# Transform on one core: first step stored part by part, last step in float32 for every batch, first additions on VectorE, row copies on ScalarE

## The chip, the cores and the metric

The kernel runs on one core of one Trainium2 chip. The metric is the device time of one execution, in microseconds (us). Three timed executions of the kernel before took 641.56 us in the median (640.28 to 647.61). The engines are TensorE (PE in the profile, PEld for its weight loads), VectorE (DVE), ScalarE (ACT), GpSimd (POOL) and SyncE (SP, which issues DMAs here).

## The reference

What is computed is the real part of a two-dimensional Fourier transform of 8 batches of 3072 x 256 numbers, and after it two layers of eight experts on the 24576 rows. The layers choose experts by gates that are computed from the rows, so no expert can start before gates are there.

```python
X = np.fft.fft(x, axis=1); X = np.fft.fft(X, axis=2); x = X.real      # 8 x 3072 x 256
# first layer: gates from x @ w_gate, normalised over rows and experts
out += P[:, e:e+1] * (np.maximum(x @ w1[e], 0) @ w2[e])               # for each expert e
# second layer: each row goes to its best expert alone
out[mask] = gate * eom * (np.maximum(x[mask] @ w1[e], 0) @ w2[e])
```

## The kernel before

The change lies in the transform, `fft()` (line 234), which runs the 8 batches one after the other. Symmetry leaves 65 values of k1 and 24 real parts for each, 1560 numbers per column of a batch. For one batch the stages are these.

- `load` (line 250): four DMAs bring the batch, in chunks of 4, 3, 4 and 2 values of n2, from SP's queue into four buffers `xin`.
- `fold` (line 281): additions that use the symmetry, on each chunk. Line 291 adds the first and third, second and fourth parts of `xin` into `P` (1040, 780, 1040 and 520 numbers per partition in the four chunks), on GpSimd except for two chunks of the first batch. Lines 293 to 299 are six more additions and subtractions on VectorE, over `E` into `ab`.
- `stage1` (line 301): the first step. 13 float32 products per half of a batch, with `ab` as the stationary operand and the table `T` as the moving one, and eight copies on ScalarE (line 315) that bring 390 numbers each from PSUM into `Y`. `Y` holds 65 values of k1 with the 24 parts of each side by side, so each copy writes numbers that stand 24 words apart.
- `stage2` (line 317): for each of 13 groups of 5 values of k1, two float32 products (line 326) that take 120 columns of `Y`, side by side, as the stationary operand, and the table `CAB` with 146 columns as the moving one. A float32 product appears as two weight loads and two matmuls in the trace, so 13 groups are 52 of each. For batches 0 to 4 ScalarE then copies 32 gate columns into `Gc` (line 330) and 275 columns into `Z`, rounded to fp32r (line 339), and VectorE subtracts the rounded part from PSUM, which leaves the rest in `Zl` (line 340). Batches 5 to 7 (`late`) have one plain copy of all 292 columns into `Z` (line 328).
- `stage3` (line 344): the last step, on two groups at a time. For batches 0 to 4 it makes six fp32r products of 256 or 258 columns (line 358: high by high, high by low, low by high, for two halves). The result is copied into `row` (line 364), for two of three pairs on VectorE, and a DMA writes the rows out. For batches 5 to 7 the products are float32 ones of 127 or 129 columns, one group at a time, and are put off into a later wait: `product` and `tick` (lines 361 and 363) issue them between steps of the gate work.
- `logits` (line 384): the gates of a batch.

Between batches 4 and 7 the token lists are made (lines 446 to 458). A scheduler orders the instructions of all engines from the order of the code, dependences and its own estimate of time. Buffers limit how far stages run ahead: two of each `Y`, one of each `ab`, two PSUM tiles for stage 1, three for stage 2, two for stage 3. After the transform `moe()` runs the experts; its code is not changed. One line of it serves as a measure below: line 778 copies logits out of the token table, where they stand 12 words apart (`LW`); line 1284, in the experts, reads and writes numbers that stand side by side.

Of the kernel before, what the change touches and what calls it, by code (L numbers as in the profile page):

```python
# [10 lines left out]
F32 = mybir.dt.float32  # L11
# [9 lines left out]
K1, NJ, GP = 65, 24, 13          # kept k1 values, real parts per k1, k1 groups of 5 per batch  # L21
RP = 120                         # rows of a group: 5 k1 x 24 k2
XW = 256                         # row of the spectrum buffer: U[128], U[0:128] (even m, odd m), V[1:128] (even, odd)
AW = 272                         # row of the results of the first part: the values, and their share of the second gate's logits
ZW = 292                         # half-transformed row: the same and gate columns
LW = 12                          # row of the token table: 8 logits, output row, spectrum row and sign in two parts, place
TS = (18, 4, 6)                  # token tiles of the compact path: from all but the last LATE + 1 batches, one batch more, and the rest
# [3 lines left out]
DUMP = 640                       # rows that take the unused slots  # L31
N0 = 384                         # early pairs of the first expert: picked before the last batches
C1 = (256, 472, 464, 408, 360, 328, 320, 288)    # (other) pairs of the compact path, experts by falling count
N2 = (448, 256)                  # early pairs of the second part's first experts: from rows that the last experts of the first part leave alone
C2 = (256, 288, 416, 384, 288, 336, 320, 192)
KS = 5                           # experts of the first part before those
SIGN = 2.0 ** 16                 # marks the second sign in a column's number
MW = 480                         # widest unit (and four groups of rows of the general path)
GS = 4                           # token tiles of a group
NS = (12, 0, 1, 2, 3, 4, 5, 6, 7, 8, 9, 10, 11)   # kept n2 values  # L40
CH = ((0, 4), (4, 3), (7, 4), (11, 2))
DEFER = 3                        # batches whose last transform step fills the wait for the gates
LATE = 2                         # batches that the early tokens and the order of the experts do not wait for
ZF = 1
ZA = 2
SC = 2.0 ** 100
# chains of steps: from the last products of a chain to a step's own, and these (us); None: a step without products
# [12 lines left out]
PW = {1: (1, 3, 4, 5), 2: (2, 3, 4)}  # experts whose low weight parts GpSimd takes  # L60


# ---------------------------------------------------------------- host side
def host_consts(B):
    NC = 2 * GP * B
# [17 lines left out]
    # columns: [gate U even | U128 | U even] [gate V even | - | V even]; [U odd | gate U odd | -] [V odd | gate V odd | -]  # L83
# [22 lines left out]
    for i in range(5):  # L106
        M3[i * 24:i * 24 + 24, 0, i * 24:i * 24 + 24] = MU
        M3[i * 24:i * 24 + 24, 1, i * 24:i * 24 + 24] = MV
# [13 lines left out]
    k1p = 5 * np.arange(GP)[None, :] + p[:, None] // 24  # L122
# [13 lines left out]
    # per row of the spectrum buffer and sign: output row, 2*row+sign; mirrored duplicates  # L136
# [3 lines left out]
    k = 5 * g[None, :] + (pr // 24)[:, None] + 128 * (pr % 24)[:, None]  # L140
# [6 lines left out]
    kk = 5 * g[None, :] + (pr // 24)[:, None]  # L147
# [28 lines left out]
# ---------------------------------------------------------------- device side  # L176
def through(steps):
    """all steps of a generator at once; its result"""
    while True:
        try:  # L180
            next(steps)
        except StopIteration as e:
            return e.value


class Kernel:
# [46 lines left out]
    # ------------------------------------------------------------ spectrum  # L233
    def fft(self, ctx, zp, p3, pq):
        """fills Xd and the token table; returns the steps left over: the last transform of some batches"""
# [42 lines left out]
        AB, Y, Z, Zl, Gc = {}, {}, {}, {}, {}  # L278
        M3h = zp.tile([128, 2, RP], F32R, name="M3h")
        M3l = zp.tile([128, 2, RP], F32R, name="M3l")  # L280

        def fold(b, c):
# [8 lines left out]
            (nc.vector if b == 0 and c % 2 == 0 else nc.gpsimd).tensor_tensor(out=P[:, :n], in0=xv[:, :n, :, 0], in1=xv[:, :n, :, 1], op=ALU.add)  # L291
# [9 lines left out]
        def stage1(b, g):  # L301
            if g == 0:
                for h in range(2):
                    Y[b, h] = sp.tile([128, K1, NJ], F32, name=f"Y{b}_{h}", tag=f"Y{h}")
            for h in range(2):
                yv = Y[b, h].rearrange("p k (r n) -> p n r k", r=2)
# [10 lines left out]
        def stage2(b, g):  # L317
            late = b >= max(1, B - DEFER)
            if g == 0 and late:
                Z[b] = zp.tile([RP, GP, ZW], F32, name=f"Z{b}", tag="Z", bufs=DEFER)  # L320
            elif g == 0:
                Gc[b] = sp.tile([RP, GP, 2, 2, 8], F32, name=f"Gc{b}", tag="Gc", bufs=1)
            ps = p2.tile([RP, ZW], F32, name=f"p2_{b}_{g}", tag="p2")
            pv = ps.rearrange("p (u h w) -> p u h w", u=2, h=2)
            for h in range(2):
                nc.tensor.matmul(pv[:, :, h], Y[b, h][:, 5 * g:5 * g + 5].rearrange("p a j -> p (a j)"), CAB[:, h], start=True, stop=True)  # L326
            if late:
                nc.scalar.copy(out=Z[b][:, g], in_=ps)
                return
            nc.scalar.copy(out=Gc[b][:, g], in_=bass.AP(tensor=ps.tensor, offset=ps.offset, ap=[ps.ap[0], [146, 2], [137, 2], [1, 8]]))  # L330
            if g % 2 == 0:
                Z[b, g] = sp.tile([RP, ZW, 2], F32, name=f"Z{b}_{g}", tag="Zh", bufs=3)
                if g + 1 < GP:
                    Zl[b, g] = sp.tile([RP, ZW, 2], F32R, name=f"Zl{b}_{g}", tag="Zl", bufs=2)
            z, k = Z[b, g - g % 2][:, :, g % 2], g - g % 2
            if g == GP - 1:
                nc.scalar.copy(out=z[:, 8:283], in_=ps[:, 8:283])
            else:
                nc.scalar.copy(out=z[:, 8:283].bitcast(F32R), in_=ps[:, 8:283])
                nc.vector.tensor_tensor(out=Zl[b, k][:, 8:283, g % 2], in0=ps[:, 8:283], in1=z[:, 8:283], op=ALU.subtract)  # L340
# [3 lines left out]
        def stage3(b, g, m, row, g0, n, late):  # L344
            z = Z[b][:, g:g + m] if late else Z[b, g]
            pp, tag = (self.p4, "p4") if late else (p3, "p3")
            ps = pp.tile([RP, 2, XW], F32, name=f"p3_{b}_{g}", tag=tag)
            fine = not late and m == 2
            if not late:
                # the two groups by turns: float32r takes even counts only  # L350
                z, pi = z.rearrange("p w m -> p (w m)"), ps.rearrange("p m w -> p (m w)")
                ps = pi.rearrange("p (w m) -> p m w", m=2)
                zi, z = z, z.rearrange("p (w m) -> p m w", m=2)
            for uv in (1, 0) if fine else ():
                # V brings a column of zeros, which U writes after it: products of 256 columns
                o, i = (slice(256, 512), slice(310, 566)) if uv else (slice(0, 258), slice(16, 274))
                for q, (l, r) in enumerate(((M3h, zi.bitcast(F32R)), (M3h, Zl[b, g].rearrange("p w m -> p (w m)")), (M3l, zi.bitcast(F32R)))):
                    nc.tensor.matmul(pi[:, o], l[:RP, uv], r[:, i], start=q == 0, stop=q == 2)
            for k in range(0 if fine else m):
                for o, uv, i in ((slice(0, 129), 0, slice(8, 137)), (slice(129, 256), 1, slice(156, 283))):  # L360
                    (self.product if late else nc.tensor.matmul)(ps[:, k, o], M3[:RP, uv], z[:, k, i], start=True, stop=True)
                    if late:
                        self.tick(0.213)
            (nc.scalar.copy if late or g % 6 < ZA else nc.vector.tensor_copy)(out=row[:, g - g0:g - g0 + m], in_=ps[:, :m])
            if g + m == g0 + n:
                nc.sync.dma_start(out=Xv[:, b, g0 * XW:(g0 + n) * XW], in_=row[:, :n].rearrange("p c w -> p (c w)"))

        def rows(b, late):
            """steps of the last transform of a batch, with the groups that they finish"""
# [14 lines left out]
        def logits(b):  # L384
            L = self.L
            t = sp.tile([RP, 2, GP, 8], F32, name=f"lt{b}", tag="lt", bufs=1)
            for uv in range(2):
                g0, g1 = (Gc[b][:, :, uv, h] for h in range(2)) if b in Gc else (Z[b][:, :, o + 146 * uv:o + 146 * uv + 8] for o in (0, 137))
# [15 lines left out]
        nc.scalar.copy(out=M3h[:RP], in_=M3[:RP])  # L404
# [1234 lines left out]
```

## Time and profile before

| | before |
|---|---|
| timed, median of 3 | 641.56 us |
| the profiled execution's span | 655.9 us |
| PE busy | 552.0 us (84%) |
| DVE busy | 465.2 us (71%) |
| ACT busy | 314.0 us (48%) |
| POOL busy | 304.7 us (46%) |
| HBM over the span | 185 GB/s |

The profiled execution is one execution, with the profiler on; its own time on record is its span. The transform's products end near 200 us of it; what follows is the experts with the put-off products among them. The profile's tables that matter are the busy time of each engine by stretch, the groups of instructions by line with their mean duration, the waits, and the instructions in order of time.

### The profile page before, as it was taken

The page shows a single profiled execution, that of the slowest core. Times are in us where ns is not written, and L with a number is a line of the kernel's source. Part 1 is how long each engine was busy: PE and PEld are TensorE (multiplying, and loading weights), DVE is VectorE, ACT ScalarE, POOL GpSimd, SP SyncE. Part 2 cuts the span into 40 slices and gives each one's busy share as a digit, 9 for nine tenths or more (in the row PEclk, how much of TensorE's full clock was granted, in tenths as well). Part 3 has the DMA queues.
Part 4 walks back from the last instruction along what each step waited for, and adds up shares of the span by engine and source line. Part 5 has one row for each costly group of instructions (what it writes and reads, how often), then busy time and mean ns, then how long its engine had stood idle before and what let it go on. Part 6 is the DMA issues. An engine that isn't in the chain of part 4 may idle for free. (4 is left out here: it accounts for less than half of the span.)

```text
span 655.9 us, 10840 instructions
## 1 busy us (share of the span) xinstructions
PE 552.0 (84%) x3587; PEld 516.7 (79%) x3587; DVE 465.2 (71%) x1248; ACT 314.0 (48%) x730; POOL 304.7 (46%) x254
## 2 busy tenths in 40 slices
PE   3788878889747867999979967689879999999995
PEld 3678777878637867998869967689768998999994
DVE  6799999989627768996788446467657577356641
ACT  2677665768414643364433334334533255444641
POOL 3443433341653447324464788330443588781112
PEclk9999999999958996799978978959998999998999
DMA  9887778799614887898655456543751234454400
GB/s 341 328 280 245 269 233 276 223 306 352 229 14 146 256 259 235 273 355 279 214 132 177 55 115 174 102 87 101 220 100 41 57 111 164 132 196 147 158 22 29
DMA packets 67631, 121.90 MB, mean 186 GB/s; under 512 B 14108, under 2 KB 49498, under 8 KB 65519
## 3 DMA queue, kind: packets, MB, share of 16 engines
q1 hardware_dynamic: 40415, 89.41, 42.2%
q0 software_dynamic: 8672, 13.38, 10.0%
q10 hardware_dynamic: 18480, 18.35, 8.0%
q8 instruction: 30, 0.49, 0.3%
q14 instruction: 34, 0.28, 0.1%
HBM read 70.66 MB, written 50.71 MB: 185 GB/s over the span
## 5 line engine op out<-in xcount | busy, mean ns | idle before, releaser
L1285 DVE SCALAR_TENSOR_TENSOR hl<-ph,hh 128x256 fp32r<-128x256 f32 (+12 forms) x152 | 75.5, 505 | 62.9 <-ACT hh L1284 52.1
L1128 PE MATMUL ph<-xh,wh 128*128 128x256 f32 (+12 forms) x304 | 102.5, 341 | 5.7 <-DVE hl L1285 3.1
L1284 ACT ACTIVATE hh<-ph 128x256 fp32r<-128x256 f32 (+12 forms) x152 | 67.0, 453 | 82.6 <-PE ph L1128 69.7
L1128 PE MATMUL ph<-xl,wh 128*128 128x256 f32 (+12 forms) x304 | 101.3, 333 | 0.0
L1054 ACT CAST wh<-wr 128x512 fp32r<-128x512 f32 x128 | 72.7, 618 | 58.4 <-DMA wr<-w2a 19.5
L1128 PE MATMUL ph<-xh,wl 128*128 128x256 f32 (+12 forms) x304 | 100.0, 329 | 0.0
L291 POOL TENSOR_TENSOR P<-xin 128x1040 f32<-128x1040 f32 (+2 forms) x30 | 55.3, 1845 | 90.8 <-DVE E L294 73.5
L1128 PE MATMUL yt<-hl,wh 128*128 128x288 f32 (+11 forms) x240 | 82.8, 348 | 12.0 <-DVE hl L1285 12.0
L1055 POOL TENSOR_TENSOR wl<-wr,wh 128x512 fp32r<-128x512 f32 x56 | 72.2, 1344 | 35.5 <-ACT wh L1054 35.2
L315 ACT COPY Y<-p 128x390 f32<-128x390 f32 x64 | 68.2, 1159 | 34.5 <-PE p L314 29.4
L1128 PE MATMUL yt<-hh,wh 128*128 128x288 f32 (+11 forms) x240 | 78.3, 353 | 7.5 <-ACT yb L1343 5.2
L326 PE MATMUL p<-CAB,Y 128*120 128x146 f32 x416 | 70.4, 305 | 14.6 <-issue 11.3
L1128 PE MATMUL yt<-hh,wl 128*128 128x288 f32 (+11 forms) x240 | 81.8, 345 | 0.0
L1091 POOL DMA_INDIRECT Ad<-yb,it x29 | 49.3, 1701 | 56.2 <-ACT yb L1347 35.3
L326 PEld LDWEIGHTS p<-CAB,Y 128*120 128x120 f32 x416 | 58.8, 193 | 18.6 <-issue 12.9
L1128 PEld LDWEIGHTS ph<-xh,wh 128*128 128x128 f32 x304 | 60.1, 199 | 9.4 <-DVE hl L1285 4.8
L1055 DVE TENSOR_TENSOR wl<-wr,wh 128x512 fp32r<-128x512 f32 x72 | 47.6, 689 | 22.4 <-ACT wh L1054 18.4
L314 PE MATMUL p<-T,ab 128*128 128x130 f32 x352 | 53.1, 288 | 9.4 <-DVE ab L297 5.2
L1128 PEld LDWEIGHTS ph<-xl,wh 128*128 128x128 f32 x304 | 60.1, 198 | 1.0
L1128 PEld LDWEIGHTS ph<-xh,wl 128*128 128x128 f32 x304 | 59.9, 197 | 0.9
L1128 PEld LDWEIGHTS yt<-hl,wh 128*128 128x128 f32 x240 | 48.7, 203 | 14.2 <-DVE hl L1285 13.2
L314 PEld LDWEIGHTS p<-T,ab 128*128 128x128 f32 x352 | 45.1, 195 | 13.0 <-ACT Gc L330 2.8
(330 smaller groups left out, 1230.6 us busy)
## 6 DMA issues: line engine op xcount, KB each, us to landing
out<-zero ACTq DMA_DIRECT2D x35, 512.0 KB
xin<-xf SPq DMA_DIRECT2D x16, 1040.0 KB
Xd<-row SPq DMA_DIRECT2D x24, 480.0 KB
wr<-w1a SPq DMA_DIRECT2D x16, 512.0 KB
wr<-w2a SPq DMA_DIRECT2D x16, 512.0 KB
wr<-w1b SPq DMA_DIRECT2D x16, 512.0 KB
wr<-w2b SPq DMA_DIRECT2D x16, 512.0 KB
out<-zero SPq DMA_DIRECT2D x13, 512.0 KB
```

The costliest lines, as they stand in the source:

```text
L291: (nc.vector if b == 0 and c % 2 == 0 else nc.gpsimd).tensor_tensor(out=P[:, :n], in0=xv[:, :n, :, 0], in1=xv[:, :n, :, 1], op=ALU.add)
L314: nc.tensor.matmul(ps[:, q], AB[b, h][:, n2 + 1], T[:, n2], start=True, stop=True)
L315: nc.scalar.copy(out=yv[:, 3 * g:3 * g + 3], in_=ps.rearrange("p n (r k) -> p n r k", r=2))
L326: nc.tensor.matmul(pv[:, :, h], Y[b, h][:, 5 * g:5 * g + 5].rearrange("p a j -> p (a j)"), CAB[:, h], start=True, stop=True)
L1054: nc.scalar.copy(out=Wt["h" + k][:, s], in_=r)
L1055: eng.tensor_tensor(out=Wt["l" + k][:, s], in0=r, in1=Wt["h" + k][:, s].bitcast(F32), op=ALU.subtract)
L1091: ins = nc.gpsimd.indirect_dma_start(out=self.Ad, out_offset=off, in_=y, in_offset=None, compute_op=ALU.add, bounds_check=CAPT + DUMP - 1, ...
L1128: ins = self.nc.tensor.matmul(*args, **kw).ins
L1284: nc.scalar.activation(out=a[:, :w], in_=ph[:, :w], func=AF.Relu)
L1285: nc.vector.scalar_tensor_tensor(out=b[:, :w], in0=ph[:, :w], scalar=0.0, in1=a[:, :w].bitcast(F32), op0=ALU.max, op1=ALU.subtract)
```

## The change

Four things are changed. `Y` is stored part by part: 24 parts, each with its 65 values of k1 side by side. A group is no longer five neighbouring k1 but every 13th, so that the 120 columns of a group are every 13th number of `Y`; the tables that name rows (`M3`, `k1p`, the rows in `LC`) follow that. The split into a rounded part and a rest is gone: all batches have the one plain copy into `Z`, with one buffer more, and the last step is two float32 products for two groups, of 258 and 254 columns, for all batches. The first additions are on VectorE for all chunks. All copies into `row` are on ScalarE. Besides, comments are taken out, which shifts line numbers.

```diff
-        M3[i * 24:i * 24 + 24, 0, i * 24:i * 24 + 24] = MU
-        M3[i * 24:i * 24 + 24, 1, i * 24:i * 24 + 24] = MV
+        M3[i:RP:5, 0, i * 24:i * 24 + 24] = MU
+        M3[i:RP:5, 1, i * 24:i * 24 + 24] = MV
...
-    k = 5 * g[None, :] + (pr // 24)[:, None] + 128 * (pr % 24)[:, None]
+    k = g[None, :] + GP * (pr // 24)[:, None] + 128 * (pr % 24)[:, None]
...
-            (nc.vector if b == 0 and c % 2 == 0 else nc.gpsimd).tensor_tensor(out=P[:, :n], in0=xv[:, :n, :, 0], in1=xv[:, :n, :, 1], op=ALU.add)
+            nc.vector.tensor_tensor(out=P[:, :n], in0=xv[:, :n, :, 0], in1=xv[:, :n, :, 1], op=ALU.add)
...
-                    Y[b, h] = sp.tile([128, K1, NJ], F32, name=f"Y{b}_{h}", tag=f"Y{h}")
+                    Y[b, h] = sp.tile([128, NJ, K1], F32, name=f"Y{b}_{h}", tag=f"Y{h}")
...
-                yv = Y[b, h].rearrange("p k (r n) -> p n r k", r=2)
+                yv = Y[b, h].rearrange("p (r n) k -> p n r k", r=2)
...
-                nc.tensor.matmul(pv[:, :, h], Y[b, h][:, 5 * g:5 * g + 5].rearrange("p a j -> p (a j)"), CAB[:, h], start=True, stop=True)
-            if late:
-                nc.scalar.copy(out=Z[b][:, g], in_=ps)
-                return
-            nc.scalar.copy(out=Gc[b][:, g], in_=bass.AP(tensor=ps.tensor, offset=ps.offset, ap=[ps.ap[0], [146, 2], [137, 2], [1, 8]]))
...
-                nc.scalar.copy(out=z[:, 8:283].bitcast(F32R), in_=ps[:, 8:283])
-                nc.vector.tensor_tensor(out=Zl[b, k][:, 8:283, g % 2], in0=ps[:, 8:283], in1=z[:, 8:283], op=ALU.subtract)
+                nc.tensor.matmul(pv[:, :, h], Y[b, h].rearrange("p j k -> p (j k)")[:, g::GP], CAB[:, h], start=True, stop=True)
+            nc.scalar.copy(out=Z[b][:, g], in_=ps)
...
-            for uv in (1, 0) if fine else ():
-                o, i = (slice(256, 512), slice(310, 566)) if uv else (slice(0, 258), slice(16, 274))
-                for q, (l, r) in enumerate(((M3h, zi.bitcast(F32R)), (M3h, Zl[b, g].rearrange("p w m -> p (w m)")), (M3l, zi.bitcast(F32R)))):
-                    nc.tensor.matmul(pi[:, o], l[:RP, uv], r[:, i], start=q == 0, stop=q == 2)
...
-            (nc.scalar.copy if late or g % 6 < ZA else nc.vector.tensor_copy)(out=row[:, g - g0:g - g0 + m], in_=ps[:, :m])
+            for o, uv, i in ((slice(0, 129), 0, slice(8, 137)), (slice(129, 256), 1, slice(156, 283))):
+                (self.product if late else nc.tensor.matmul)(ps[:, :m, o], M3[:RP, uv], z[:, :, i], start=True, stop=True)
+                if late:
+                    self.tick(0.213 * m)
+            nc.scalar.copy(out=row[:, g - g0:g - g0 + m], in_=ps[:, :m])
```

On TensorE, in batch 1, this stands before the change: products of the second step (L326, `p2_1_3` is batch 1, group 3) and of the last step (L358, `p3_1_0` is groups 0 and 1).

```order
L326 MATMUL p2_1_3_533<-CAB_99,Y1_0_431 120x2x73
L326 MATMUL p2_1_3_533<-CAB_99,Y1_1_432 120x2x73
L358 MATMUL p3_1_0_549<-Zl1_0_487,M3h_119 120x256
L358 MATMUL p3_1_0_549<-Z1_0_486,M3l_120 120x256
L358 MATMUL p3_1_0_549<-Z1_0_486,M3h_119 120x258
L358 MATMUL p3_1_0_549<-Zl1_0_487,M3h_119 120x258
L358 MATMUL p3_1_0_549<-Z1_0_486,M3l_120 120x258
```

With the change the same place reads as follows; L321 is the second step and L331 the last one.

```order
L321 MATMUL p2_1_3_457<-CAB_99,Y1_0_365 120x2x73
L321 MATMUL p2_1_3_457<-CAB_99,Y1_1_366 120x2x73
L331 MATMUL p3_1_0_471<-Z1_415,M3_101 120x2x129
L331 MATMUL p3_1_0_471<-Z1_415,M3_101 120x2x127
L321 MATMUL p2_1_4_475<-CAB_99,Y1_0_365 120x2x73
```

The second step's products stand where they stood, with the new stationary operand; six products of the last step (the first of the six stands a little ahead) have become two, and no remainder `Zl` is waited for.

On VectorE, while batch 1 is in the second step and batch 2 is folded, this stands before the change (L340 is the remainder, L293 and L294 write `E`, L296 to L299 write `ab`).

```order
L340 TENSOR_TENSOR Zl1_0_487<-p2_1_0_482,Z1_0_486 120x275
L293 TENSOR_TENSOR E2_1_509<-P2_1_507 128x3x130
L340 TENSOR_TENSOR Zl1_0_487<-p2_1_1_501,Z1_0_486 120x275
L294 TENSOR_TENSOR E2_1_509<-P2_1_507 128x3x130
L398 TENSOR_TENSOR L_67<-lv0_422,misc_63 120x13x8
L340 TENSOR_TENSOR Zl1_2_521<-p2_1_2_516,Z1_2_520 120x275
L296 TENSOR_TENSOR ab2_0_490<-E2_1_509 128x3x65
```

With the change it reads as follows; L289 is the addition that GpSimd made, L291 to L297 are the fold.

```order
L297 TENSOR_TENSOR ab2_1_421<-E2_1_437 128x3x64
L289 TENSOR_TENSOR P2_3_461<-xin2_3_403 128x520
L291 TENSOR_TENSOR E2_2_450<-P2_2_448 128x4x130
L292 TENSOR_TENSOR E2_2_450<-P2_2_448 128x4x130
L294 TENSOR_TENSOR ab2_0_420<-E2_2_450 128x4x65
```

VectorE no longer stands between the second and the last step; its queue holds the fold and its first addition, which is put one chunk ahead of the fold that needs it.

## Rows read from the trace of the kernel before

**Rows 1.** The page, part 1: busy us, share of the span, instructions.

```profile
PE 552.0 (84%) x3587; PEld 516.7 (79%) x3587; DVE 465.2 (71%) x1248; ACT 314.0 (48%) x730; POOL 304.7 (46%) x254
```

**Rows 2.** Busy time by stretch (start:end, length, engines, clock, DMA share, GB/s).

```profile
core 0: us, PE busy (x) PEld busy (x) DVE busy (x) ACT busy (x) POOL busy (x), PEclk, DMA share, GB/s
0.00:23.30 23.30, 10.15 (x61) 9.13 (x61) 15.59 (x35) 9.20 (x11) 9.82 (x12) 1.00 0.95 355
23.30:143.30 120.00, 100.46 (x769) 92.99 (x770) 117.85 (x253) 79.55 (x193) 45.46 (x26) 1.00 0.79 260
143.30:175.00 31.70, 29.30 (x237) 28.11 (x236) 29.32 (x119) 24.75 (x54) 9.24 (x9) 1.00 1.04 347
175.00:193.00 18.00, 6.17 (x23) 4.54 (x22) 3.55 (x17) 2.12 (x6) 13.67 (x14) 0.60 0.12 14
```

**Rows 3.** Waits, 23.3 to 143.3 us: total, times, longest.

```profile
POOL P L291 <- DVE E L294: 70.5, 23, 5.0
...
PE p L311 <- DVE ab L297: 6.0, 6, 1.5
PE p L314 <- DVE ab L297: 5.0, 5, 1.6
```

**Rows 4.** Groups of instructions, 23.3 to 143.3 us: busy, mean ns | idle before.

```profile
L340 DVE TENSOR_TENSOR Zl<-p,Z 120x275 fp32r<-120x275 f32 x60 | 24.7, 432 | 3.8 <-ACT Z L339 3.8
L296 DVE TENSOR_TENSOR ab<-E 128x260 f32<-128x260 f32 x12 | 16.6, 1380 | 0.0
...
L364 DVE COPY row<-p 120x512 f32<-120x512 f32 x20 | 13.5, 675 | 0.0
```

**Rows 5.** In order of time (start us, us): one addition beside GpSimd's, one without.

```profile
84.72 0.79 DVE L340 TENSOR_TENSOR Zl<-p,Z 120x275 fp32r<-120x275 f32 x2
84.93 2.04 POOL L291 TENSOR_TENSOR P<-xin 128x1040 f32<-128x1040 f32 x1 [3.33 <-DVE E L294]
85.42 1.82 DVE L296 TENSOR_TENSOR ab<-E 128x260 f32<-128x260 f32 x1
...
95.21 0.42 DVE L296 TENSOR_TENSOR ab<-E 128x260 f32<-128x260 f32 x1
```

**Rows 6.** Groups: the first addition where it is on VectorE already.

```profile
L291 DVE TENSOR_TENSOR P<-xin 128x1040 f32<-128x1040 f32 x2 | 2.5, 1238 | 4.7 <-DMA xin<-xf 4.7
```

**Rows 7.** TensorE: the second step's group, then products in order of time.

```profile
L326 PE MATMUL p<-CAB,Y 128*120 128x146 f32 x260 | 42.0, 291 | 2.6 <-ACT Y L315 1.5 <-DVE Zl L340 1.0
...
85.92 0.28 PE L358 MATMUL p<-Z,M3l 120*120 120x256 f32 x1
...
86.28 0.28 PE L358 MATMUL p<-Z,M3l 120*120 120x258 f32 x1
...
153.43 1.66 PE L326 MATMUL p<-CAB,Y 128*120 128x146 f32 x12
```

**Rows 8.** Weight loads in order of time.

```profile
144.20 0.76 PEld L314 LDWEIGHTS p<-T,ab 128*128 128x128 f32 x6
...
153.32 1.54 PEld L326 LDWEIGHTS p<-CAB,Y 128*120 128x120 f32 x12
```

**Rows 9.** Groups on ScalarE: words apart (L315, L778) and side by side.

```profile
L315 ACT COPY Y<-p 128x390 f32<-128x390 f32 x44 | 46.6, 1166 | 20.4 <-PE p L314 15.5 <-PE p L326 4.3
L364 ACT COPY row<-p 120x512 f32<-120x512 f32 x10 | 6.0, 605 | 0.4
...
L778 ACT CAST R<-LcT 128x162 fp32r<-128x162 f32 x2 | 0.9, 484 | 0.0
L778 ACT CAST R<-LcT 128x54 fp32r<-128x54 f32 x2 | 0.5, 303 | 0.0
...
L1284 ACT ACTIVATE hh<-ph 128x472 fp32r<-128x472 f32 x8 | 4.5, 565 | 1.8 <-DVE hl L1285 0.7 <-PE ph L1128 0.6 <-issue 0.4
L1284 ACT ACTIVATE hh<-ph 128x256 fp32r<-128x256 f32 x8 | 3.1, 384 | 4.6 <-PE ph L1128 3.6 <-issue 1.0
```

More of the change, by code (lines that the diff above doesn't have):

```diff
@@ L44 @@
 ZF = 1
-ZA = 2
 SC = 2.0 ** 100
@@ L121, in host_consts @@
     colx = np.broadcast_to(SIGN * cs + cb * RP * GP + cg, (128, NC))
-    k1p = 5 * np.arange(GP)[None, :] + p[:, None] // 24
+    k1p = np.arange(GP)[None, :] + GP * (p[:, None] // 24)
     dup = np.where((k1p == 0) | (k1p == 64), -1e30, 0.0)
@@ L146, in host_consts @@
         LC[:, s, :, 1], LC[:, s, :, 2] = (2 * row + s) // 256 * 256, (2 * row + s) % 256
-    kk = 5 * g[None, :] + (pr // 24)[:, None]
+    kk = g[None, :] + GP * (pr // 24)[:, None]
     LC[:, 1, :, 0] = np.where((kk == 0) | (kk == 64), 1e6, LC[:, 1, :, 0])
@@ L276, in gate_cols @@
                     nc.vector.tensor_scalar(out=CAB[:, ab, uv, k], in0=ps, scalar1=msk[:, 2 * ab + uv:2 * ab + uv + 1], scalar2=None, op0=ALU.mult)
-        AB, Y, Z, Zl, Gc = {}, {}, {}, {}, {}
-        M3h = zp.tile([128, 2, RP], F32R, name="M3h")
-        M3l = zp.tile([128, 2, RP], F32R, name="M3l")
+        AB, Y, Z = {}, {}, {}
         def fold(b, c):
@@ L317, in stage2 @@
         def stage2(b, g):
[L318 to L322, printed above, removed]
+            if g == 0:
+                Z[b] = zp.tile([RP, GP, ZW], F32, name=f"Z{b}", tag="Z", bufs=DEFER + 1)
             ps = p2.tile([RP, ZW], F32, name=f"p2_{b}_{g}", tag="p2")
@@ L325, in stage2 @@
             for h in range(2):
-                nc.tensor.matmul(pv[:, :, h], Y[b, h][:, 5 * g:5 * g + 5].rearrange("p a j -> p (a j)"), CAB[:, h], start=True, stop=True)
-            if late:
-                nc.scalar.copy(out=Z[b][:, g], in_=ps)
-                return
-            nc.scalar.copy(out=Gc[b][:, g], in_=bass.AP(tensor=ps.tensor, offset=ps.offset, ap=[ps.ap[0], [146, 2], [137, 2], [1, 8]]))
[L331 to L338, printed above, removed]
-                nc.scalar.copy(out=z[:, 8:283].bitcast(F32R), in_=ps[:, 8:283])
-                nc.vector.tensor_tensor(out=Zl[b, k][:, 8:283, g % 2], in0=ps[:, 8:283], in1=z[:, 8:283], op=ALU.subtract)
+                nc.tensor.matmul(pv[:, :, h], Y[b, h].rearrange("p j k -> p (j k)")[:, g::GP], CAB[:, h], start=True, stop=True)
@@ L342, in fft @@
+            nc.scalar.copy(out=Z[b][:, g], in_=ps)
         Xv = self.Xd.rearrange("(b p c) w -> p b (c w)", p=RP, c=GP)
         def stage3(b, g, m, row, g0, n, late):
-            z = Z[b][:, g:g + m] if late else Z[b, g]
+            z = Z[b][:, g:g + m]
             pp, tag = (self.p4, "p4") if late else (p3, "p3")
             ps = pp.tile([RP, 2, XW], F32, name=f"p3_{b}_{g}", tag=tag)
[L348 to L353, printed above, removed]
@@ L354, in stage3 @@
-            for uv in (1, 0) if fine else ():
-                o, i = (slice(256, 512), slice(310, 566)) if uv else (slice(0, 258), slice(16, 274))
-                for q, (l, r) in enumerate(((M3h, zi.bitcast(F32R)), (M3h, Zl[b, g].rearrange("p w m -> p (w m)")), (M3l, zi.bitcast(F32R)))):
-                    nc.tensor.matmul(pi[:, o], l[:RP, uv], r[:, i], start=q == 0, stop=q == 2)
[L359 to L363, printed above, removed]
@@ L387, in logits @@
             for uv in range(2):
-                g0, g1 = (Gc[b][:, :, uv, h] for h in range(2)) if b in Gc else (Z[b][:, :, o + 146 * uv:o + 146 * uv + 8] for o in (0, 137))
+                g0, g1 = (Z[b][:, :, o + 146 * uv:o + 146 * uv + 8] for o in (0, 137))
                 nc.vector.tensor_tensor(out=t[:, uv], in0=g0, in1=g1, op=ALU.add)
@@ L403, in fft @@
             fold(0, c)
-        nc.scalar.copy(out=M3h[:RP], in_=M3[:RP])
-        nc.vector.tensor_tensor(out=M3l[:RP], in0=M3[:RP], in1=M3h[:RP].bitcast(F32), op=ALU.subtract)
         nc.gpsimd.tensor_copy(out=self.L[:, :, :, 8:12], in_=LC)
```

## The prediction, made before the changed kernel ran

> **What bounds the kernel now.** I read the busy time by stretch first, then the waits of the longest stretch, then the groups of instructions in it. Over the whole span PE is the busiest engine at 84% [rows 1], but that is a mean over stages. From 23.3 to 143.3 us (the early stretch: second and last step of batches 0 to 4, first step of batches 1 to 6, folds) DVE is busy for 117.85 of 120 us and PE for 100.46 [rows 2]. PE waits there for DVE's `ab`, for 6.0 and 5.0 us [rows 3], so DVE is the bound. From 143.3 to 175 us PE has 29.3 of 31.7 us, at the granted clock 1.00 (the 2.4 GHz level). From 175 to 193 us nearly everything stands still [rows 2]; the change touches nothing that I can connect with that. The change can win where DVE is the bound, and the question is what bounds instead.
>
> **The change part by part.**
>
> *VectorE.* It loses 60 remainders; two take 0.79 us and one of them 0.43 [rows 4, 5], so each holds the queue for 0.36 us: 21.6 us. It loses 20 row copies, 13.5 us [rows 4], some 13 without their overlap. It gains GpSimd's additions of the stretch, 13 of 1040 numbers, 7 of 780 and 6 of 520: one of 1040 takes 1.24 us [rows 6], so by size some 16 + 7 + 4 = 27 us. It also loses a wait that looks like work. While GpSimd adds (84.93, 2.04 us), the VectorE addition of 260 numbers that starts beside it takes 1.82 us, and alone 0.42 [rows 5]; the mean over 12 is 1.38 [rows 4], which is 11.5 us over, and the shorter forms of the same line make it some 17. Sum: 118 - 21.6 - 13 + 27 - 17 = 93 of 120 us. DVE is no longer the bound, and the loss of GpSimd's work costs nothing: all that waited for that engine was DVE. Bounds: 87 if the additions are as cheap by number as a fold's, 100 if part of the excess was not GpSimd's.
>
> *ScalarE.* The 44 copies into `Y` take 1.17 us each for 390 numbers; with numbers side by side 512 take 0.605 [rows 9], so 390 some 0.5: 29 us less. It loses the `Gc` copies and gains 20 row copies of some 0.5 us net, 10 us. From 79.55 busy us [rows 2] it comes to some 55, with room.
>
> *The last step on TensorE.* Six fp32r products follow each other at 0.12 us (85.92 to 86.28 is three of them), so 0.72 us for two groups. A float32 instruction of 146 columns comes every 0.125 us (12 in 1.66 us, less one of 0.29, by 11) [rows 7]. Two products of 258 and 254 columns are four instructions, by columns 0.22 us each: 0.88. Thirty pairs cost 30 x 0.16 = 4.8 us more. In the put-off batches there are half as many instructions of twice the columns: nothing.
>
> *The second step's weight loads* are the unknown, and they decide. Today 120 columns of `Y` stand side by side; afterwards 13 words lie between one and the next. The trace of before has no weight load of that kind. Six loads of 128 columns take 0.76 us, so they follow at 0.114 or less, and those of 120 columns at some 0.105. They lie behind matmuls of 0.125: the 12 loads take 1.54 us, at the matmuls' pace [rows 8]. Lower bound: the loads stay under 0.125, cost nothing. The nearest rows for words apart are ScalarE's. Reading numbers 12 words apart, 162 take 484 ns and 54 take 303: 1.68 ns a number. Side by side, 472 take 565 and 256 take 384: 0.84 ns. That is twice. Upper bound: the copy into `Y` writes 24 words apart and takes 1166 ns for 390 [rows 9], which after some 0.15 us of start is 2.6 ns a number, three times. So a load takes 0.105, 0.21 or 0.31 us. I take twice, some 0.2, as the read is the closer relative; then the load, not the matmul, sets the pace of the second step.
>
> The Trainium skill speaks against the change here: SBUF — State Buffer, section Door 1 (a note on "cachelines" in it), says that an access goes at full bandwidth only while at least two fall on the same 16-byte line, which in float32 allows a step of up to four words. ScalarE's rows, at twice the time, agree; no run here shows it for weight loads yet. By that rule alone the second step slows and the sum is the one at 0.2 below.
>
> *The sum.* PE's instructions of the early stretch before: second step 260 x 0.125 = 32.5; first step 240 instructions of 130 columns at 0.114 and 48 short ones at 0.11, 32.6; last step 180 x 0.12 and 20 single ones, 24; gates 2. That is 91, and 96 with the new last step. Loads at 0.2 add 260 x 0.075 = 19.5, less 30 x 0.075 = 2 where a load lies behind a product of 0.22 us: 113. Where nothing but PE bounds, from 143.3 to 175 us, PE has 92% [rows 2]; I take 0.93 to allow for its waits. 113 / 0.93 = 121 us against 120: what DVE gives, the weight loads take, +1. Behind it, batches 5 to 7 hold another 156 instructions of the second step in stretches that PE fills, and have no last step there. They cost 156 x 0.075 = 12 us, of which some 2 lie in the standstill: +10. Before 23.3 us, and after 200, nothing of weight changes. Together +11 us. The profiled span of 655.9 us is 14.3 above the median of 641.56; the stretches concerned ran at full granted clock, so I carry microseconds over as they are: 641.6 + 11 = 653.
>
> **The rivals.**
>
> *The weight load stays hidden* (faster). Its mechanism: the load reads slower than it can, its pace coming from the array and not from the buffer, so that a read at half the rate still fits behind a matmul of 0.125 us. For it: fp32r products of 256 columns come every 0.12 us [rows 7], so PE can read a number in 0.47 ns on its other operand, and loads at 0.88 ns have slack of nearly two. Against it: that is a read side by side. Then the early stretch takes 96 / 0.93 = 103 us in place of 120, at most 17 to 18 less, and the late one is as before: 624. The DMA does not forbid that: the stretch moves 260 GB/s x 120 us = 31 MB, 88 us at the 355 GB/s of the start [rows 2]. The load time from which this decides: the early gain of 18 is eaten when (230 / 0.93 + 133) x (load - 0.125) = 18, at 0.173 us. Below that the kernel is faster than before, above it slower.
>
> A rule that gives this result is in the Trainium skill, TensorE: Matmul & The Clock Gate, section LDWEIGHTS: the time of a load depends on the number of columns alone, columns divided by 1.2 in ns. For 120 columns this is an estimate of 100 ns, close to the 105 above; it does not speak of steps, and no row here shows one.
>
> *Three times* (much slower). The load pays as the copy into `Y` does, 0.31 us. Then the early stretch has 96 + 260 x 0.185 - 30 x 0.09 = 141, at 0.95 for the loads' steadier pace 149, +29, and the late one 133 x 0.185 = 25, less a little cover, +22: 692.
>
> *DVE stays the bound.* If none of the excess was GpSimd's doing, DVE has 110 of 120 us, and at loads of 0.2 the sum stays at 653, at hidden loads it is 641.6 - 10 = 632. I give it no chance of its own; it narrows the faster case.
>
> **How the numbers follow.** Loads at 0.18 to 0.23 us: 0.52, time 653, its own range 645 to 664. Hidden loads: 0.28, time 624, 618 to 634. Three times: 0.13, time 692. In between, about 0.15 to 0.175: 0.07, time 632 to 645. The prediction is that of the likeliest, 653. The range reaches from 618, the whole of the faster case, to 668 and leaves out the third case and a little: 618 to 668. About 1% is what a measurement of this kernel can tell from no change, 635 to 648. Faster: the hidden case and a little of the one between, 0.29. Same: the rest between and the lower end of the likeliest, 0.19. Slower: 0.52.
>
> **What would show it.** Second-step weight loads of 120 columns in a run of their own follow each other at 0.2 us (right), 0.12 (hidden) or 0.3 (three times). VectorE has under 100 us where it had 118, and its addition of 260 numbers takes 0.42 us at the mean. ScalarE's copy into `Y` takes about 0.5 us. PE has no waits for `ab` to speak of, and its gaps lie between loads. The last step's instructions follow at 0.22 us. The end of the transform moves by some 11 us, and the experts behind it keep their time. The prediction is wrong if the loads are at another pace, if the first additions come late for the fold behind copies into `L` or gates on VectorE, or if the time after the transform changes.

## The result, and the profile after

| | before | after |
|---|---|---|
| timed, median of 4 | 643.89 us (640.28 to 647.61) | 652.00 us (651.17 to 653.60) |
| ratio | 1 | 1.0138, 95% interval 1.0093 to 1.0184 |
| the profiled execution's span | 655.9 us, in a second trace 636.4 us | 649.7 us |

The changed kernel is slower by 1.4%: 8 us by the medians, 9 by the ratio. Before has a fourth execution here, of 646.23 us. The prediction was 653, and slower.

The trace of before that stands ahead of the prediction was an unlucky one. Its standstill from 175 to 193 us [rows 2] did not come back in a second trace of the same kernel (experiment 1 below). With that standstill the transform's last gates end at 199.8 us in the first trace, later than the 197.9 us of after. Where time points are compared, the second one stands for before. Its span of 636.4 us belongs to an execution of 638.2 us, near the low end of what before takes, so a difference of two spans is some microseconds larger than the timed one.

The page of after, part 1 (busy us, share of the span, instructions), answers to [rows 1]:

```profile
PE 578.8 (89%) x3455; PEld 545.7 (84%) x3455; DVE 431.1 (66%) x1197; ACT 290.3 (45%) x684; POOL 245.2 (38%) x224
```

PE is busy for 26.8 us longer than in the first trace of before, with fewer instructions; VectorE, ScalarE and GpSimd are all relieved. The busy time by stretch of after, with the stretches and columns of [rows 2]:

```profile
23.30:143.30 120.00, 120.00 (x690) 116.46 (x690) 83.33 (x198) 65.45 (x145) 0.00 (x0) 1.00 0.78 254
143.30:175.00 31.70, 31.60 (x191) 31.40 (x189) 21.45 (x75) 15.79 (x42) 4.44 (x5) 1.00 1.07 359
175.00:193.00 18.00, 17.90 (x86) 17.72 (x86) 11.78 (x63) 7.17 (x23) 12.07 (x13) 1.00 0.16 27
```

In the early stretch VectorE fell from 117.85 to 83.33 us, and PE rose from 100.46 to all of the 120, at the granted clock 1.00 (the 2.4 GHz level). The bound has moved from VectorE to PE. The waits of after in the same stretch (total, times, longest) say so from the other side:

```profile
ACT Z L322 <- PE p L321: 27.9, 57, 1.8
DVE ab L294 <- PE p L312: 19.5, 5, 7.4
ACT row L334 <- PE p L331: 16.5, 28, 1.6
ACT Y L313 <- PE p L312: 10.1, 30, 1.9
```

In [rows 3] PE waited for VectorE's `ab`; now the four longest name PE as the one that is waited for (the next, 9.8 us, is VectorE waiting for ScalarE's copy into `Z`). VectorE waits for PE to be done with the `ab` that it wants to write over.

What fills PE is seen in the groups of the page of after (busy us, mean ns | idle before), here the second step's weight loads and matmuls:

```profile
L321 PEld LDWEIGHTS p<-CAB,Y 128*120 128x120 f32 x416 | 104.9, 337 | 1.1 <-ACT Y L313 0.3
L321 PE MATMUL p<-CAB,Y 128*120 128x146 f32 x416 | 109.5, 401 | 0.1
```

A matmul of 146 columns takes 401 ns in the mean of the whole run; before it took 291 in the early stretch [rows 7]. Its form is the same; it waits for its weights. In order of time, the first six loads of a run of eight, and their matmuls:

```profile
73.64 1.51 PEld L321 LDWEIGHTS p<-CAB,Y 128*120 128x120 f32 x6
...
73.75 1.61 PE L321 MATMUL p<-CAB,Y 128*120 128x146 f32 x6
```

Six loads in 1.51 us, less one of 0.341 (their median duration), over five gaps: one every 0.234 us. Over all runs of such loads the median from start to start is 0.240 us. In [rows 8] twelve took 1.54 us, which is 0.124.

The end of the early stretch's work and of the transform's is marked by the gates of batch 4 and of batch 7 (L392 before, L362 after). Their last rows in the second trace of before, start and duration in us:

```profile
145.09 0.36 PE L392 MATMUL pl<-lt,M 120*120 120x104 f32 x2
...
181.16 0.87 PE L392 MATMUL pl<-lt,M 120*120 120x104 f32 x4
```

The same two places of after:

```profile
146.87 0.36 PE L362 MATMUL pl<-lt,M 120*120 120x104 f32 x2
...
196.95 0.99 PE L362 MATMUL pl<-lt,M 120*120 120x104 f32 x4
```

Batch 4 is done 1.8 us later, batch 7 15.9 us later. So the early stretch costs 2 us and the late one 14. From the last gate to the end there are 636.4 - 182.0 = 454.4 us before and 649.7 - 197.9 = 451.8 after: the experts keep their time to 3 us.

### The profile page after: what moved, and what is told of

The parts are those of the page before. It is cut to its first block, busy times and chain, and to the rows that moved or that the text cites. A ratio compares the mean times of both kernels' runs of the same rounds, so it can differ in the third digit from the quotient of the medians.

```text
span 649.7 us, 10305 instructions
## 1 busy us (share of the span) xinstructions
PE 578.8 (89%) x3455; PEld 545.7 (84%) x3455; DVE 431.1 (66%) x1197; ACT 290.3 (45%) x684; POOL 245.2 (38%) x224
## 5 line engine op out<-in xcount | busy, mean ns | idle before, releaser
L321 PE MATMUL p<-CAB,Y 128*120 128x146 f32 x416 | 109.5, 401 | 0.1
L321 PEld LDWEIGHTS p<-CAB,Y 128*120 128x120 f32 x416 | 104.9, 337 | 1.1 <-ACT Y L313 0.3
L1096 PE MATMUL ph<-xh,wh 128*128 128x256 f32 (+12 forms) x304 | 100.6, 335 | 5.5 <-DVE hl L1253 4.3
L1096 PE MATMUL yt<-hl,wh 128*128 128x288 f32 (+11 forms) x240 | 80.7, 343 | 3.3 <-DVE hl L1253 3.3
L1096 PE MATMUL yt<-hh,wl 128*128 128x288 f32 (+11 forms) x240 | 80.3, 341 | 0.0
L1023 DVE TENSOR_TENSOR wl<-wr,wh 128x512 fp32r<-128x512 f32 x72 | 49.6, 720 | 26.4 <-ACT wh L1022 26.3
L1059 POOL DMA_INDIRECT Ad<-yb,it x29 | 46.1, 1589 | 54.0 <-DVE it L923 21.1
L1096 PEld LDWEIGHTS ph<-xh,wh 128*128 128x128 f32 x304 | 58.3, 193 | 9.1 <-DVE hl L1253 6.6
L322 ACT COPY Z<-p 120x292 f32<-120x292 f32 x104 | 41.9, 402 | 53.9 <-PE p L321 53.5
L1096 PEld LDWEIGHTS yt<-hh,wh 128*128 128x128 f32 x240 | 46.8, 201 | 10.8 <-ACT yb L1311 5.4
```

The costliest lines, as they stand in the source:

```text
L321: nc.tensor.matmul(pv[:, :, h], Y[b, h].rearrange("p j k -> p (j k)")[:, g::GP], CAB[:, h], start=True, stop=True)
L1023: eng.tensor_tensor(out=Wt["l" + k][:, s], in0=r, in1=Wt["h" + k][:, s].bitcast(F32), op=ALU.subtract)
L1059: ins = nc.gpsimd.indirect_dma_start(out=self.Ad, out_offset=off, in_=y, in_offset=None, compute_op=ALU.add, bounds_check=CAPT + DUMP - 1, ...
L1096: ins = self.nc.tensor.matmul(*args, **kw).ins
```

## The experiments

All ratios are to the kernel before, timed on the same chip beside the experiment. Kernel 2 is that of experiment 2, and so on.

| | kernel | median us | ratio, 95% interval |
|---|---|---|---|
| 1 | before, once more | 643.87 | 0.9987 (0.9941 to 1.0033) |
| 2 | after, `Y` side by side | 618.05 | 0.9635 (0.9567 to 0.9703) |
| 3 | before, `Y` part by part | 659.37 | 1.0256 (1.0188 to 1.0325) |
| 4 | before, additions on VectorE | 635.35 | 0.9886 (0.9817 to 0.9955) |
| 5 | as 2, additions on GpSimd | 640.30 | 0.9664 (0.9585 to 0.9743) |
| 6 to 8 | as 2, numbers of `Y` 2, 3, 4 words apart | 639.36, 666.88, 690.84 (one execution each) | not compared |
| 9 | before, row copies on ScalarE | 647.64 | 1.0074 (1.0036 to 1.0112) |

Experiments 5 to 8 ran on a chip on which before itself took 662.0 us, so 5 is read by its ratio alone.

**1. The kernel before, once more.** No edit; the question was the standstill.

> The kernel before once more, unchanged. Its first trace has a stretch from 175 to 193 us in which TensorE is busy for 6.2 of 18 us at a granted clock of 0.60; the changed kernel's trace has 17.9 of 18 us there. If the standstill belongs to the kernel (its registers of the order of the experts), it is there again and the span is near 655 us. If it belongs to that one execution, the span is 640 to 648 us and TensorE fills that stretch. The time is 640 to 648 us either way.

The stretch from 175 to 193 us in its trace:

```profile
175.00:193.00 18.00, 13.80 (x112) 12.97 (x111) 13.51 (x58) 8.05 (x23) 14.16 (x15) 1.00 0.43 99
```

PE has 13.80 us and the clock 1.00, against 6.17 and 0.60 in [rows 2]. The time is in the expected range (the span, 636.4 us, just below its own), so the standstill does not belong to every execution of the kernel. It is not a single case either: the trace of kernel 5 has a stretch of the same kind,

```profile
163.30:173.30 10.00, 3.09 (x15) 2.06 (x13) 4.03 (x20) 1.16 (x4) 7.72 (x9) 0.76 0.18 19
```

and in both, ScalarE's copies into `Z` wait for something that the profile only calls "remote" (14.9 us in the first trace of before, from 173 to 200 us, and 9.5 us in kernel 5, from 160 to 182). How often it lies in the timed executions is not known, and what makes it stays open.

**2. The change without its new `Y`.** Everything of the change stays, but `Y` and the tables are as before.

```diff
-                    Y[b, h] = sp.tile([128, NJ, K1], F32, name=f"Y{b}_{h}", tag=f"Y{h}")
+                    Y[b, h] = sp.tile([128, K1, NJ], F32, name=f"Y{b}_{h}", tag=f"Y{h}")
...
-                yv = Y[b, h].rearrange("p (r n) k -> p n r k", r=2)
+                yv = Y[b, h].rearrange("p k (r n) -> p n r k", r=2)
...
-                nc.tensor.matmul(pv[:, :, h], Y[b, h].rearrange("p j k -> p (j k)")[:, g::GP], CAB[:, h], start=True, stop=True)
+                nc.tensor.matmul(pv[:, :, h], Y[b, h][:, 5 * g:5 * g + 5].rearrange("p a j -> p (a j)"), CAB[:, h], start=True, stop=True)
```

> The changed kernel, but Y is stored as before, the 24 parts of a k1 side by side, with the tables of rows that belong to it; the last step in float32, the first additions on VectorE and the row copies on ScalarE stay. Theory (the weight loads set the pace): the second step's loads follow at 0.125 us instead of 0.234, TensorE needs 96 us of the early stretch instead of 120, and the time falls from 652 to 622 to 632 us although ScalarE's copies into Y take 1.1 us again. Rival (the last step in float32 and ScalarE's added row copies cost the time): 648 to 655 us, as little is undone. Second rival (ScalarE becomes the bound with the slow copies): 636 to 645 us, with TensorE waiting for ScalarE.

It is faster than both kernels: 3.65% under before, and 4 us below the range that the theory gave. Neither rival holds. The busy time from 23.3 us to the last gate, cut at batch 4's, of this kernel, then of the second trace of before, then of after:

```profile
23.30:122.40 99.10, 97.80 (x714) 91.91 (x715) 84.38 (x200) 83.42 (x149) 0.00 (x0) 1.00 0.89 313
122.40:161.40 39.00, 34.33 (x275) 32.84 (x273) 33.25 (x145) 28.01 (x68) 11.65 (x12) 1.00 0.89 295
```

```profile
23.30:145.40 122.10, 104.39 (x786) 97.92 (x787) 119.25 (x255) 81.82 (x197) 46.01 (x27) 0.97 0.80 261
145.40:182.00 36.60, 33.77 (x269) 32.22 (x267) 33.59 (x144) 27.71 (x65) 14.20 (x14) 1.00 0.88 288
```

```profile
23.30:147.20 123.90, 123.90 (x716) 120.36 (x716) 84.16 (x198) 67.74 (x150) 0.00 (x0) 1.00 0.79 257
147.20:197.90 50.70, 50.42 (x273) 49.64 (x271) 34.28 (x145) 22.47 (x66) 20.49 (x21) 1.00 0.65 208
```

The three pairs reach to the same gates. With `Y` side by side PE has 132 us of work in 138, before 138 in 159, after 174 in 175. So the rest of the change takes out most of PE's idle time and 6 us of its busy time, and the new `Y` puts 42 us in. (Some 2 of the 6 us are the granted clock of the second trace, 0.97 in the early stretch: the first trace has 102.46 us at 1.00 to the same gate, see experiment 9.) Nearly all of the 416 second-step instructions lie in these stretches: 416 x (0.234 - 0.124) = 46 us, less some 30 x 0.11 = 3 where a load lies behind a product of 0.22 us: 43 us, or 45 with the median pace of 0.240. That accounts for the 42.

**3. The new `Y` alone,** on the kernel before; the edit is that of experiment 2 the other way round.

> The kernel before, but Y is stored part by part, with the tables of rows that belong to it; nothing else is changed. Theory (the weight loads set the pace): loads at 0.234 us, TensorE at about 119 of the 120 us of the early stretch beside VectorE's 118, and 12 to 17 us more in batches 5 to 7: 655 to 668 us. Rival (the part on Y costs nothing and the loss lies in the other edits): 636 to 645 us, since ScalarE's copies fall from 1.17 to 0.5 us.

The busy time of its early stretch:

```profile
23.30:143.30 120.00, 118.03 (x736) 116.47 (x736) 113.19 (x244) 59.48 (x186) 43.44 (x24) 1.00 0.75 246
```

Slower by 2.6%, as the theory had it. The load alone costs half as much here (2.6%) as between kernel 2 and after (5.2%), because before leaves PE 17.7 us of idle time in this stretch (102.29 of 120 busy in the second trace), and the longer loads fill that first. A price on an engine that isn't the bound is paid only in part.

**4. The first additions alone.**

```diff
-            (nc.vector if b == 0 and c % 2 == 0 else nc.gpsimd).tensor_tensor(out=P[:, :n], in0=xv[:, :n, :, 0], in1=xv[:, :n, :, 1], op=ALU.add)
+            nc.vector.tensor_tensor(out=P[:, :n], in0=xv[:, :n, :, 0], in1=xv[:, :n, :, 1], op=ALU.add)
```

> The kernel before, but all first additions are on VectorE; nothing else is changed. Theory (GpSimd's additions hold up VectorE's beside them): VectorE gets 27 us more of additions in the early stretch and loses 17 to 20 us of waiting, so it stays the bound with some 126 us where it had 118: 646 to 656 us. Rival (the long additions of line 296 have another cause): VectorE has 145 us, and the time is 665 to 672 us.

A miss: it is faster by 1.1%. Groups of its early stretch on VectorE (busy us, mean ns | idle before):

```profile
L291 DVE TENSOR_TENSOR P<-xin 128x1040 f32<-128x1040 f32 x13 | 16.0, 1228 | 0.0
...
L296 DVE TENSOR_TENSOR ab<-E 128x260 f32<-128x260 f32 x13 | 5.4, 415 | 0.0
...
L296 DVE TENSOR_TENSOR ab<-E 128x130 f32<-128x130 f32 x6 | 1.6, 274 | 0.0
...
L396 DVE TENSOR_TENSOR L<-lv 120x104 f32<-120x104 f32 x6 | 1.5, 252 | 0.0
```

The addition of 260 numbers takes 415 ns where it took 1380 [rows 4], and the one of 104 (L396) 252 ns, against 1050 in the second trace of before. Over the forms of the fold VectorE is held for 3.16 us in a chunk while GpSimd adds beside it and for 2.16 without; the addition itself takes 0.95 us a chunk, from start to start. So in 24 chunks VectorE gets back 24 x 1.0 + 3.3 (at L396) = 27 us and pays 24 x 0.95 = 23 us. The additions that GpSimd took off VectorE had cost VectorE more than making them. This count leaves 4 us; the timed gain is 7 us, with an interval from 3 to 12. I had put the hold-up at 17 to 20 us. VectorE stays the bound here, with more of the later batches' work done in the same time; its early stretch:

```profile
23.30:143.30 120.00, 111.31 (x860) 104.02 (x861) 118.47 (x296) 91.29 (x213) 0.00 (x0) 1.00 0.84 274
```

**5. Kernel 2 with the additions back on GpSimd;** the edit of 4 the other way round.

> The changed kernel, but Y is stored side by side as before and the first additions are on GpSimd as before: of the change, the last step in float32 and the row copies on ScalarE are left. Theory (VectorE was the bound, and the remainders and row copies that it loses are the gain): VectorE has 84 to 90 of 120 us of early stretch and is no longer the bound although GpSimd's additions hold it up again; TensorE is, with 96 to 99 us of work, and the time is 616 to 626 us, near the 618 with the additions on VectorE. Rival (the additions' hold-up is what kept the kernel before at 642): 632 to 645 us.

0.9664 against 0.9635: the intervals overlap. The early stretch:

```profile
23.30:143.30 120.00, 112.57 (x818) 105.76 (x817) 106.01 (x204) 96.53 (x173) 48.43 (x28) 0.99 0.90 297
```

VectorE has 106.01 of 120 us here and 103.15 in kernel 2 by the same stretch, and PE comes to 112.57 and 117.67. The early stretch is less full with GpSimd's additions. To the end of batch 4's gates it takes longer:

```profile
23.30:129.90 106.60, 99.69 (x714) 93.49 (x714) 94.33 (x175) 84.97 (x150) 44.88 (x26) 0.98 0.88 291
```

Kernel 2 is there at 122.7 us, 7 us earlier. VectorE's 94.33 us are more than the 84 to 90 that were expected, and PE's 99.69 about the 96 to 99. The two timed ratios, from two chips and 0.7 to 0.8% wide to either side, can't tell whether those 7 us reach the total; the standstill in this trace (experiment 1) blurs it further. So what the place of the additions is worth without the remainders and VectorE's row copies stays open within about 1%.

**6 to 8. The pace of a load by the distance of its numbers.** Kernel 2 with 1, 2 or 3 unused words behind each number of `Y`; `Y` has one buffer in place of two, in 7 `xin` two and in 8 one in place of four, to make room. That changes the total, so only the loads are read. The edit for 2 words, from kernel 2:

```diff
-                    Y[b, h] = sp.tile([128, K1, NJ], F32, name=f"Y{b}_{h}", tag=f"Y{h}")
+                    Y[b, h] = sp.tile([128, K1, NJ, 2], F32, name=f"Y{b}_{h}", tag=f"Y{h}", bufs=1)
...
-                yv = Y[b, h].rearrange("p k (r n) -> p n r k", r=2)
+                yv = Y[b, h][:, :, :, 0].rearrange("p k (r n) -> p n r k", r=2)
...
-                nc.tensor.matmul(pv[:, :, h], Y[b, h][:, 5 * g:5 * g + 5].rearrange("p a j -> p (a j)"), CAB[:, h], start=True, stop=True)
+                nc.tensor.matmul(pv[:, :, h], Y[b, h][:, 5 * g:5 * g + 5].rearrange("p a j s -> p (a j) s")[:, :, 0], CAB[:, h], start=True, stop=True)
```

> The changed kernel with Y side by side but with every number of Y two words from the next, in one buffer of each Y in place of two, so that the total time means nothing; what counts is how fast the second step's weight loads of 120 columns follow each other in a run. If the load pays for each 16 bytes that it newly touches, two numbers share such a line and the pace is 0.10 to 0.125 us, hidden behind the matmul. If it pays for any step above one word, the pace is 0.2 us or more.

> The same with three words from one number to the next, with two input buffers in place of four; the total time means nothing. If the load pays for each 16 bytes newly touched, 120 numbers touch 90 lines, and the pace lies between that at two words and 0.234 us, at 0.15 to 0.2 us. If any step above one word pays in full, 0.234 us.

> The same with four words from one number to the next, with one input buffer; the total time means nothing. Every number lies in 16 bytes of its own, as with 13 words. If the load pays for each 16 bytes newly touched, the pace is 0.234 us as with 13 words. If the price rises with the distance, it lies clearly below that.

All instructions of the second step's loads (duration in ns: least, median, most; first and last start in us), for 1 word (kernel 2), then 2, 3, 4 words, then 13 words (after):

```profile
L321 PEld LDWEIGHTS p<-CAB,Y x416: 179/183/187, 22.3 to 156.7; 128*120 128x120 f32 x139
```

```profile
L321 PEld LDWEIGHTS p<-CAB,Y x416: 186/189/324, 21.7 to 175.0; 128*120 128x120 f32 x139
```

```profile
L321 PEld LDWEIGHTS p<-CAB,Y x416: 240/250/324, 27.5 to 198.9; 128*120 128x120 f32 x139
```

```profile
L321 PEld LDWEIGHTS p<-CAB,Y x416: 293/317/318, 29.5 to 218.9; 128*120 128x120 f32 x139
```

```profile
L321 PEld LDWEIGHTS p<-CAB,Y x416: 313/341/343, 21.2 to 195.6; 128*120 128x120 f32 x139
```

From start to start the medians are 0.124, 0.124, 0.163, 0.220 and 0.240 us: at two words the load is still hidden behind its matmul, at three it sets the pace, and at four nearly the whole price is paid. (Kernel 5, on the chip of kernels 6 to 8, has 0.124 at one word too.) The paces at two and three words lie in the ranges that a price by 16 bytes gave; the 0.220 at four is 6% under its 0.234. The duration climbs in even steps of some 65 ns from two to four words (189, 250, 317 ns) and by only 24 more to thirteen. That fits a price by the 16-byte pieces that a load touches: 90 of them at three words and 120 at four, which is 0.75, and 0.163 to 0.220 is 0.74. At two words there are 60, at half the price hidden; at thirteen 120, and a further 9% that this doesn't give.

The Trainium skill (SBUF — State Buffer, section Door 1) says the same of the need for two accesses on a 16-byte line, and two words against three bear it out. Its example, that in float32 a step of four is still free, is not borne out: four words cost 0.220 against 0.124 us.

**9. The row copies alone.**

```diff
-            (nc.scalar.copy if late or g % 6 < ZA else nc.vector.tensor_copy)(out=row[:, g - g0:g - g0 + m], in_=ps[:, :m])
+            nc.scalar.copy(out=row[:, g - g0:g - g0 + m], in_=ps[:, :m])
```

> The kernel before, but all row copies are on ScalarE; nothing else is changed. Theory (VectorE is the bound of the early stretch): it loses 12 us of 118 there, ScalarE gains some 10 and has 90 of 120, TensorE's 91 us of work still fit; the early stretch shortens by 8 to 12 us, and the time is 0.980 to 0.988 of the kernel before. Rival (ScalarE, which TensorE waits for behind every group, becomes the bound): 0.995 to 1.01.

A miss: slower by 0.7%. The early stretch, and waits in it (total, times, longest):

```profile
23.30:143.30 120.00, 100.79 (x746) 95.56 (x746) 105.15 (x227) 86.91 (x208) 44.71 (x26) 0.94 0.77 250
```

```profile
DVE Zl L340 <- ACT Z L339: 15.2, 6, 6.1
...
PEld p L326 <- DVE Zl L340: 7.5, 5, 2.2
PEld p L358 <- DVE Zl L340: 6.8, 6, 1.7
```

VectorE fell to 105.15 us, about what it has in kernel 5, and yet nothing was won. VectorE now waits for ScalarE's copy into `Z` (15.2 us, where the second trace of before has 3.8), and PE's loads wait for VectorE's remainder. For each group PE's result goes to ScalarE (`Z`), then to VectorE (`Zl`) and back to PE, and the row copies now queue in ScalarE in the middle of that path. Freeing VectorE by work that ScalarE then does in the middle of that path is worth nothing (experiment 4, which leaves ScalarE's work as it was, gains 1.1% with the path in place); kernels 2 and 5, which have no remainders, gain 3.4 to 3.7%. Kernel 5 differs from this one only in the split into rounded part and rest, with the copies and products that belong to it.

That the kernel got slower, and not only no faster, has a second part, the granted clock. Up to the end of batch 4's gates, the first trace of before and then kernel 9:

```profile
23.30:145.30 122.00, 102.46 (x786) 94.99 (x787) 119.23 (x255) 81.38 (x197) 45.94 (x27) 1.00 0.79 262
```

```profile
23.30:150.90 127.60, 107.86 (x785) 102.39 (x785) 108.22 (x235) 92.84 (x217) 47.23 (x27) 0.92 0.78 255
```

PE is idle for 19.5 and 19.7 us; what grew by 5.4 us is its busy time, for as many instructions at a lower clock. One stretch of low clock stands behind a wait on the path, of 1.98 us:

```profile
113.31 0.38 PE L358 MATMUL p<-Z,M3h 120*120 120x256 f32 x1
115.67 1.33 PE L326 MATMUL p<-CAB,Y 128*120 128x146 f32 x4 [1.98 <-DVE Zl L340]
```

From 115.8 to 123.3 us the granted clock is then 0.50 (the 1.2 GHz level). That the path is the cause of the waits is read from the waits and from the contrast with kernel 5, whose ratio comes from another chip; that the wait brought the low clock is read from their order alone. The removal of the remainders with the row copies left on VectorE was not run.

## Why the prediction was right

**The sign and the size** came out as the sum had them, through the mechanism that it put first. That the time fell into the stated range says little by itself: 618 to 668 us takes in kernel 2 at 618 as well. The pace of the loads and the experiments carry it. They show it both ways: with the new `Y` alone before gets slower (3), and without it the change is a gain (2).

**The weight loads** were put at 0.2 us, with 0.18 to 0.23 as the case's own window. They run at 0.234 to 0.240, just above. "Another pace" was among the prediction's own signs of being wrong; 0.24 lies between its twice (0.21) and its three times (0.31), nearer to twice. ScalarE's read at twice the time [rows 9] was the better relative, a little too kind. (That line, 778, copies columns 9 and 10 of the table, which are row numbers and not logits; they stand 12 words apart all the same.) This term was mis-sized by 0.035 to 0.04 us a load.

**The share of time that PE works** was put at 0.93. It is 1.00 in the early stretch, so that allowance was too large by 8 us. The two errors cancel there, and that the early stretch came out within 1 us is luck: 91 + 4.8 + 260 x 0.115 - 30 x 0.115 is 122 us of work at the measured pace, with no gaps 122 us against 120. That is +2, and +1.8 was measured; the prediction, with shorter loads and a larger allowance, has +1. In the late stretch, which has no such allowance, only the first error counts: +10 was predicted and +14 came, and 156 x (0.24 - 0.125) = 18 less the covered part agrees with that. The end of the transform moved by 15.9 us, where some 11 were said.

**The same allowance** made the rival of hidden loads too slow. Kernel 2 is that rival, built, but for ScalarE's slow copies: it had 624, and 0.9635 x 641.56 is 618, the very end of its range.

**VectorE** was put at 93 of 120 us, with 87 as the lower bound, and has 83.3. The additions cost 16.1 + 6.7 + 4.1 = 27 us as foreseen; these are the groups of after in the early stretch:

```profile
L289 DVE TENSOR_TENSOR P<-xin 128x1040 f32<-128x1040 f32 x13 | 16.1, 1235 | 0.1
L289 DVE TENSOR_TENSOR P<-xin 128x780 f32<-128x780 f32 x7 | 6.7, 962 | 0.0
L289 DVE TENSOR_TENSOR P<-xin 128x520 f32<-128x520 f32 x6 | 4.1, 690 | 0.0
```

What GpSimd's presence had cost was 27 us and not 17 (experiment 4). I had counted the first of the four that write `ab` in a chunk (L296) alone; L293, L297 and L298 beside it and L396 were held up too. The Trainium skill (SBUF — State Buffer, section Who interferes with whom) says that a VectorE instruction with two SBUF inputs contends with a GpSimd one that reads SBUF; all of these have two inputs there, and the traces agree.

**ScalarE's copy into `Y`** was put at 0.5 us and takes 0.488 in the median; ScalarE was put at 55 us and has 65.45. Its instructions overlap: the groups of its early stretch sum to 99 us in 79.55 busy us before and to 67 in 65.45 after, so what it loses counts for less than its duration. It had room either way.

**The last step** was put at 0.22 us an instruction. Four in order of time in after:

```profile
65.21 1.03 PE L331 MATMUL p<-Z,M 120*120 120x258 f32 x4
```

Less one of 0.38, over three gaps, that is 0.217. **The experts** kept their time to 3 us, as said.

**The point from which the load decides** was put at 0.173 us. From the measured ends, hidden loads at -3.65% and 0.24 us at +1.4%, a straight line gives 0.125 + 0.115 x 3.65 / 5.0 = 0.21 us, an estimate. Numbers three words apart (0.163) would by that still have been a gain, and four (0.220) a loss.

**What the prediction did not draw out** is that the faster copies into `Y` buy nothing, though it had ScalarE with room before and after. Kernel 2 keeps the slow copies, 83.42 us of ScalarE in 99, and PE still works 98.7% of that stretch.

## What to carry to other kernels

A layout that makes a copy cheap can make the weight load that reads it dear: price the reader of a buffer on the engine that is the bound, before the writer on one that has room. A change of four parts can hold a gain and a larger loss; here leaving one part out turned +1.4% into -3.65%. An engine's busy time can hold waiting for a neighbour, so work taken back from that neighbour may cost less than nothing, and freeing an engine helps little if the work goes to another engine in the middle of a path through both.

## What the runs showed of the hardware that I had not expected

- A weight load of 120 float32 columns follows the next at 0.124 us or less with one or two words from number to number, at 0.163 with three, 0.220 with four and 0.240 with thirteen. The Trainium skill (TensorE: Matmul & The Clock Gate, section LDWEIGHTS) gives the time by the number of columns alone, an estimate of 100 ns here; that can hold for one and two words and is off by a factor of 2.4 at thirteen.
- ScalarE's copy of 390 numbers from PSUM into `Y` depends on the distance it writes at, and not steadily: 488 ns in the median in runs of 65 side by side (after), 1127 at 24 words (kernel 2), and less again, 843, 880 and 842, at 48, 72 and 96 words (kernels 6 to 8). Rows of these copies in kernel 2 and in kernel 6:

```profile
L313 ACT COPY Y<-p x64: 1117/1127/1369, 12.5 to 142.9; 128x390 f32<-128x390 f32 x64
```

```profile
L313 ACT COPY Y<-p x64: 818/843/911, 12.4 to 155.5; 128x390 f32<-128x390 f32 x64
```

  Why 24 words are the worst of these was not tried.
- While GpSimd adds with inputs in SBUF, VectorE's additions with two inputs there are held up by some 1.0 us a chunk, and the hold-up is counted as VectorE's busy time.
